# Windowed attention before two feed-forward layers: keys transposed straight into twelve pieces, scores masked and reduced for a duo at once

## The chip, the cores and the metric

The kernel runs on one core of one Trainium2 chip. A core has TensorE (PE) for matrix products, VectorE (DVE), ScalarE (ACT) and GpSimd (POOL) for element-wise work, and SyncE (SP), whose queue issues the transfers from and to memory. Products land in PSUM, eight banks of 512 fp32 values in each of 128 partitions; everything else lies in SBUF. The metric is the device time of one execution in microseconds: the median before is 644.8 us over three runs (640.82 to 644.95).

## The reference

Two batches of 8 heads, 768 tokens, 64 values a head. Each query sees the keys less than 16 tokens away, and beside them 24 summary keys, one for each block of 32 tokens: the maximum over the block, with log 32 added to its score; the summary value is the mean.

```python
k_sum = k.reshape(B, H, nb, block, D).max(axis=3)
v_sum = v.reshape(B, H, nb, block, D).mean(axis=3)
scores_l = scale * np.matmul(q, k.transpose(0, 1, 3, 2))
mask_l = np.abs(pos[:, None] - pos[None, :]) < window
scores_s = scale * np.einsum('bhsd,bhnd->bhsn', q, k_sum) + np.log(block)
scores_all = np.concatenate([np.where(mask_l, scores_l, -1e9), scores_s], axis=-1)
a = np.exp(scores_all - np.max(scores_all, axis=-1, keepdims=True))
a = a / (np.sum(a, axis=-1, keepdims=True) + 1e-09)
out = np.matmul(a, np.concatenate([v, v_sum], axis=2))
# then, on 1536 tokens x 512: h = relu(x @ w_in); x = h*h @ w_out  (512 -> 2048 -> 512)
# and: h = x @ w_in2; g = P(h) / Q(h); out = g @ w_out2            (512 -> 2048 -> 512)
```

The weights come as 8-byte numbers, whose two words ACT, DVE and POOL turn into a high and a low fp32 part; each product is three matmuls (high by high, high by low, low by high).

## The kernel before, in words

Attention works in **duos**: one pair of heads by 256 queries, four chunks (`c`) of 64 queries, the two heads side by side in 128 partitions. A batch is 12 duos in three groups of 256 tokens; a group's four duos give the 512 input rows of a feed-forward chunk of 256 tokens. There are 24 duos.

The keys of a head pair are loaded with token `p*6 + r` in partition `p` (L258), laid out anew by DVE or ACT (`k_rel`, R and A in the order below), transposed on PE six times 128 x 128 (`k_tr`, t), copied by ACT into a linear row of 768 tokens (`k_lin`, l), and from there by DVE or ACT into six overlapping windows `kt` of 184 columns, 160 window tokens with the 24 summary keys between them (`k_put`, c, C, B). The block maxima are taken from the linear row (L361).

A duo then goes through these steps. `d_t` and `d_z` (q, z) transpose and copy the queries; `d_s` (s) makes 4 x 120 scores in a PSUM bank; `d_m` (m) adds the mask, scales, negates and takes the minimum, one fused DVE instruction and a read-out a chunk (L444); `d_e` (e) is the exponential on ACT; `d_r` (r) the row sum, plus 1e-9, and reciprocal on DVE; `d_n` (n) the normalization on POOL; `d_p`, `d_b` (p, b or f) transpose and copy the weights; `d_o` (o) multiplies by the values; `d_x`, `d_y` (x, y) split the output into high and low parts, the input of the first layer (L546). `s_add` and `v_sum` (S, V) make the summary values on POOL and PE. T, D, W are the three steps that decode a piece of a weight.

The order of the first six duos and of the first weights is written out by hand (`START`, L22 to 27) and kept in that order on every engine; the loads that come first are listed in `LOADS`. What stands outside it, the constants of `build_consts` and all transfers, is placed by a scheduler that simulates the program. After the start the remaining duos are mixed into the first layer's steps. SP's queue issues all transfers in its order. The layers' passes: `FS` (L520) splits the first layer's 16 blocks into 5 and 11, and the first five run chunk by chunk beside attention.

Of the kernel before, what the change touches and what calls it, by code (L numbers as in the profile page):

```python
# [30 lines left out]
def tile_window_attention_moe_moe(  # L31
# [120 lines left out]
    TR = S // P  # L152
    TV = 8
    VP = S // TV
    bw = ap.tile([VP, LO + NB], F32, name="bw", bufs=1)
    qz = [ap.tile([P, 4, 2, LO], F32, name=f"qz{j}", bufs=1) for j in range(2)]
    kss = [ap.tile([P, NB], F32, name=f"kss{j}", bufs=1) for j in range(NP)]
    kt = [ap.tile([P, NQ, NKEY], F32, name=f"kt{j}", bufs=1) for j in range(NP)]
    vn = [[ap.tile([HK, 2, 2 * P], F32, name=f"vn{j}{i}", bufs=1) for i in range(2)] for j in range(2)]


    lins = [acc[:, j * KC * G:j * KC * G + S + LO] for j in (3, 2, 1, 0)]
# [4 lines left out]
    kst = const.tile([P, TR, 4, D], F32, tag="xh2", name="kst")  # L167
    vst = const.tile([P, 4, TV, D], F32, tag="xl2", name="vst")[0:VP]
# [17 lines left out]
    masks = {}  # L186

    def build_consts():
        make_identity(nc, ident)
        for lin in lins:  # L190
            nc.vector.memset(lin[:, 0:WIN], 0.0)
            nc.vector.memset(lin[:, WIN + S:], 0.0)
        for z in qz:
            nc.vector.memset(z[0:D, :, 1], 0.0)
            nc.vector.memset(z[D:P, :, 0], 0.0)
        m0 = ap.tile([P, 4, HK], F32, tag="pr", name="mask", bufs=NPR)
        m0 = m0.rearrange("p c t -> p (c t)")[:, 0:NKEY]
        nc.vector.memset(m0, 0.0)
        for c0, j0, n in ((0, 0, LO), (LO + NB, LO, WT - LO)):
            nc.gpsimd.affine_select(  # L200
                out=m0[:, c0:c0 + n], in_=m0[:, c0:c0 + n], pattern=[[1, n]],
                compare_op=ALU.is_ge, fill=NEG, base=j0 - 1, channel_multiplier=-1,
            )
            nc.gpsimd.affine_select(
                out=m0[:, c0:c0 + n], in_=m0[:, c0:c0 + n], pattern=[[-1, n]],
                compare_op=ALU.is_ge, fill=NEG, base=2 * WIN - 1 - j0, channel_multiplier=1,
            )
        nc.vector.memset(m0[:, LO:LO + NB], SC * math.log(BLK))

        mid = [ap.tile([P, HK], F32, name=f"mask_mid{h}", bufs=1) for h in range(2)]  # L210
        for h in range(2):
            for e in range(2):
                nc.vector.tensor_copy(
                    mid[h][e * LO:(e + 1) * LO], m0[h * LO:(h + 1) * LO, h * LO:h * LO + HK]
                )
        m1 = ap.tile([P, HK], F32, name="mask_first", bufs=1)
        nc.vector.tensor_copy(m1, mid[0])
        nc.vector.memset(m1[:, 0:WIN], NEG)
        m2 = ap.tile([P, HK], F32, name="mask_last", bufs=1)
        nc.vector.tensor_copy(m2, mid[1])  # L220
        nc.vector.memset(m2[:, HK - WIN:], NEG)
        masks.update({(i, h): mid[h] for i in range(NQ) for h in range(2)})
        masks[0, 0] = m1
        masks[NQ - 1, 1] = m2
        nc.vector.memset(bw, 1.0 / BLK)
        for sgn, base in ((1, 0), (-1, BLK - 1)):
            for c0 in (0, LO):
                nc.gpsimd.affine_select(
                    out=bw[:, c0:c0 + NB], in_=bw[:, c0:c0 + NB], pattern=[[-sgn * BLK, NB]],
                    compare_op=ALU.is_ge, fill=0.0, base=base - (sgn < 0) * (TV - 1),  # L230
                    channel_multiplier=sgn * TV,
                )
        nc.vector.memset(bw[:, NB:LO], 0.0)
# [3 lines left out]
    NPR = 3  # L237
# [7 lines left out]
    tog = [0]  # L245

    def early():

        tog[0] += 1
        return wp.tile([P, 2 * DM], F32, tag=("wh", "wl")[tog[0] % 2], name="early")  # L250
# [4 lines left out]
    def e_load(p):  # L255

        t = early()[:, 0:2 * TR * D]
        nc.sync.dma_start(out=t.rearrange("p (h c) -> p h c", h=2), in_=rows(k[0], 2 * p, 2, TR))  # L258
        ksrc[p] = t.rearrange("p (h r d) -> p h r d", r=TR, d=D)

    def s_load(bb, h, t):
# [3 lines left out]
            out=t.rearrange("p h r d -> p h (r d)"), in_=rows(v[bb], h, n, TV)  # L265
# [6 lines left out]
    def s_add(t, to=1):  # L272

        n = TV // 2
        while n >= to:
            for h in range(0, t.shape[1], 2):
# [8 lines left out]
    def k_rel(p, copy):

        t = early()[:, 0:2 * TR * D].rearrange("p (r h d) -> p r h d", r=TR, d=D)
        copy(out=t.rearrange("p r h d -> p h r d"), in_=ksrc[p])
        ksrc[p] = t

    late = tc.keep_in_program_order

# [20 lines left out]
    def v_load(g, hh, j):  # L313
# [5 lines left out]
        for dst, lo, n in ((t[0:LO, 0], t0, LO), (t[LO + NB:HK, 0], t0 + LO, BLK),  # L319
# [7 lines left out]
            for r, s, m in segs:  # L327
# [593 lines left out]
```

## Time and profile before

| | |
|---|---|
| runs, median (three) | 644.8 us (640.82 to 644.95) |
| profiled execution, its own time | 643.41 us |
| its span from first to last instruction | 641.3 us |
| PE busy | 613.1 us (96%) |
| DVE busy | 415.1 us (65%) |
| ACT busy | 408.2 us (64%) |
| POOL busy | 351.2 us (55%) |
| mean granted TensorE clock | 0.989 of full speed |

Busy time is the time in which an engine has an instruction under way. A span is cut into stages with different limits, so the shares above do not tell by themselves which engine decides; the rows further down cut it. The time of the profiled execution and its span differ by the 2.1 us that lie around the instructions.

### The profile page before, as it was taken

Reading aid. Unit: us, or ns where it says so; the run is one execution under the profiler, and the core shown is the slowest. Engines: PE = TensorE matmul, PEld = TensorE weight load, DVE = VectorE, ACT = ScalarE, POOL = GpSimd, SP = SyncE. Lnnn points to the kernel's source line nnn. Section 1 sums busy time; section 2 is a strip of 40 time slices with the busy share of each in tenths; the row PEclk is TensorE's granted clock in tenths of the full one; section 3 lists DMA queues with packets and bytes.
Section 4 is the critical chain, followed back from the end, with each engine's and each line's share of the span. In section 5 each row is a group of like instructions: output and inputs, shape, how many; then the busy total and the mean of one; then the engine's idle time right before and its main releaser. Section 6 shows DMA issues by size and latency. Waiting matters only on the chain.

```text
span 641.3 us, 9799 instructions
## 1 busy us (share of the span) xinstructions
PE 613.1 (96%) x3476; PEld 518.5 (81%) x3476; DVE 415.1 (65%) x850; ACT 408.2 (64%) x771; POOL 351.2 (55%) x363
## 2 busy tenths in 40 slices
PE   3788899999999999999999999999999999999996
PEld 3777788999998778888888888788888888888885
DVE  5788786764767652111126799988766977766672
ACT  5577675765666632222245799888878788777761
POOL 2548755543677742322266799955445765544441
PEclk9689999999999999999999999999999999999999
DMA  9856955221555640000005543310000000001011
GB/s 231 212 136 167 247 153 106 63 47 27 167 178 182 196 132 0 2 1 0 1 0 165 164 127 103 103 62 2 1 0 1 33 2 1 1 19 47 0 66 65
DMA packets 64783, 51.48 MB, mean 80 GB/s; under 512 B 40160, under 2 KB 57568, under 8 KB 64736
## 3 DMA queue, kind: packets, MB, share of 16 engines
q1 hardware_dynamic: 64736, 50.87, 28.3%
q8 instruction: 27, 0.44, 0.3%
q14 instruction: 20, 0.16, 0.1%
HBM read 47.71 MB, written 3.15 MB: 79 GB/s over the span
## 4 chain that ended last, share of the span: by engine, by line
PE 50%; DVE 7%; ACT 2%; POOL 2%; issue 1%; DMA 1%; DVEq 0%; POOLq 0%; ACTq 0%; SPq 0%
PE y L633 25%; PE h L546 25%; DVE wdec L131 2%; POOL wl L145 1%; POOL sl L610 1%; DVE h L595 1%; ACT wdec L120 1%; DMA wraw<-in_moe_w_out_dram 1%; DVE q L592 1%; DVE wdec L130 1%; DVE p L598 1%; DVE p L580 1%; DVE acc L659 1%; DVE p L579 1%; ACT sh L609 1%
## 5 line engine op out<-in xcount | busy, mean ns | idle before, releaser
L546 PE MATMUL h<-xh,wh 128*128 128x512 f32 (+1 forms) x444 | 162.3, 366 | 3.1 <-DVE r L576 1.6
L546 PE MATMUL h<-xh,wl 128*128 128x512 f32 (+1 forms) x444 | 161.1, 363 | 0.7 <-POOL wl L145 0.7
L546 PE MATMUL h<-xl,wh 128*128 128x512 f32 (+1 forms) x444 | 161.2, 363 | 0.0
L610 POOL TENSOR_TENSOR sl<-r,sh 128x512 fp32r<-128x512 f32 (+1 forms) x63 | 69.1, 1098 | 108.0 <-ACT sh L609 100.3
L567 POOL TENSOR_TENSOR q<-q,u 128x512 f32<-128x512 f32 x48 | 63.6, 1325 | 77.8 <-ACT q L564 75.5
L145 POOL TENSOR_TENSOR wl<-wdec,wh 128x512 fp32r<-128x512 f32 x64 | 86.5, 1360 | 27.5 <-ACT wh L144 24.9
L546 PEld LDWEIGHTS h<-xh,wh 128*128 128x128 f32 x444 | 83.4, 188 | 18.5 <-DVE r L576 2.3
L546 PEld LDWEIGHTS h<-xh,wl 128*128 128x128 f32 x444 | 83.4, 188 | 15.1 <-POOL wl L145 1.1
L576 DVE TENSOR_TENSOR r<-r,h 128x512 f32<-128x512 f32 (+1 forms) x63 | 35.0, 557 | 92.3 <-ACT r L559 92.1
L546 PEld LDWEIGHTS h<-xl,wh 128*128 128x128 f32 x444 | 83.5, 188 | 13.7
L633 PE MATMUL y<-sh,wh 128*128 128x512 f32 (+1 forms) x252 | 86.0, 344 | 0.8 <-ACT sh L609 0.8
L633 PE MATMUL y<-sh,wl 128*128 128x512 f32 (+1 forms) x252 | 85.1, 340 | 0.0
L633 PE MATMUL y<-sl,wh 128*128 128x512 f32 (+1 forms) x252 | 78.7, 341 | 0.2
L610 POOL TENSOR_TENSOR sl<-p,sh 128x512 fp32r<-128x512 f32 x48 | 64.9, 1352 | 21.1 <-ACT sh L609 17.1
L633 PE MATMUL y<-wl,sh 128*128 128x512 f32 x192 | 75.0, 390 | 0.0
L633 PE MATMUL y<-wh,sh 128*128 128x512 f32 x192 | 74.5, 390 | 0.0
L633 PE MATMUL y<-wh,sl 128*128 128x512 f32 x192 | 73.6, 389 | 0.0
L131 DVE SCALAR_TENSOR_TENSOR wdec<-wraw,wdec 128x512 int32<-128x512 int32 x64 | 64.7, 1014 | 1.4
L130 DVE TENSOR_SCALAR wdec<-wdec 128x512 int32<-128x512 int32 x64 | 46.0, 718 | 25.3 <-ACT wdec L120 25.2
L609 ACT CAST sh<-r 128x512 fp32r<-128x512 f32 (+1 forms) x63 | 32.4, 514 | 42.0 <-PE y L633 39.4
L559 ACT ACTIVATE r<-h 128x512 f32<-128x512 f32 (+1 forms) x63 | 31.0, 493 | 44.1 <-PE h L546 24.4
L144 ACT CAST wh<-wdec 128x512 fp32r<-128x512 f32 x64 | 39.3, 620 | 26.9 <-DVE wdec L131 26.8
(98 smaller groups left out, 1123.6 us busy)
## 6 DMA issues: line engine op xcount, KB each, us to landing
wraw<-in_moe_w_in_dram SPq DMA_DIRECT2D x32, 512.0 KB, 3.9
wraw<-in_moe_w_out_dram SPq DMA_DIRECT2D x32, 512.0 KB, 3.4
out_dram<-acc SPq DMA_DIRECT2D x12, 256.0 KB, 2.1
acc<-in_q_dram SPq DMA_DIRECT2D x10, 256.0 KB, 5.3
vn<-in_v_dram SPq DMA_DIRECT2D x20, 96.0 KB, 2.5
early<-in_k_dram SPq DMA_DIRECT2D x4, 384.0 KB, 4.9
early<-in_v_dram SPq DMA_DIRECT2D x4, 384.0 KB, 8.1
kst<-in_k_dram SPq DMA_DIRECT2D x8, 192.0 KB, 4.2
```

Of the source, the lines that this page charges most:

```text
L120: x = nc.scalar.activation(out=f32(t), in_=f32(r[:, :, 1]), func=AF.Prelu, scale=2.0 ** -112, alpha=-(2.0 ** 32))
L130: nc.vector.tensor_single_scalar(out=t, in_=t, scalar=3, op=ALU.logical_shift_left)
L131: nc.vector.scalar_tensor_tensor(out=t, in0=low, scalar=29, in1=t, op0=ALU.logical_shift_right, op1=ALU.bitwise_or)
L144: nc.scalar.copy(out=th[:, j], in_=t)
L145: nc.gpsimd.tensor_tensor(out=tl[:, j], in0=t, in1=f32(th[:, j]), op=ALU.subtract)
L546: nc.tensor.matmul(hq[g][:, 0:n], lhsT=w[:, 0, ws], rhs=x[:, part, ts], start=(part == 0 and j == 0), stop=(part == KC - 1 and j == 2),)
L559: nc.scalar.activation(out=r, in_=h, func=AF.Relu)
L567: nc.gpsimd.tensor_tensor(out=q_, in0=q_, in1=u_, op=ALU.mult)
L576: nc.vector.tensor_tensor(out=eq[g], in0=eq[g], in1=h, op=ALU.mult)
L609: nc.scalar.copy(out=sh[:, 0:n], in_=e)
L610: nc.gpsimd.tensor_tensor(out=sl[:, 0:n], in0=e, in1=f32(sh[:, 0:n]), op=ALU.subtract)
L633: nc.tensor.matmul(o, lhsT=lt, rhs=rt, start=(f == 0 and j == 0 and d * m % 512 == 0), stop=(f == FS[ps] - 1 and j == 2 and (d + 1) * m % ...
```

## The change

Keys are loaded with token `p*8 + r` in partition `p`, into partitions 2 to 97 of a tile whose partitions 0, 1 and 96 to 99 are zeroed first. Eight transposes of 100 columns give, in two banks, the tokens with 16 zeros before and after them. Two copies a pair, one for each bank, write from PSUM straight into twelve pieces of 96 window tokens, with the 24 summary keys behind them (120 columns); the linear row is gone, and the block maxima are taken from the pieces. The scale goes into the query copies. A duo's scores are masked by one addition of 480 elements from PSUM, and one reduction takes the four maxima, negated. The 1e-9 stands in a padded column of the score tile. Values are loaded in two transfers a tile for three, into slots of the weight pool. In `START` the copies of the second bank (k) are added and DVE and ACT exchange the first two relayouts.

```diff
-    "R1 A0 t0 R3 t1 q0 l0 l1 q1 S0 A2 c0 z0 t2 S1 s0 z1 c1 m0 T0 D0 l2 s1 q2 B0 q3 e0 V0 z2 "
...
+    "R0 A1 t0 R3 t1 q0 l0 k0 l1 k1 q1 S0 A2 c0 z0 t2 S1 s0 z1 c1 m0 T0 D0 l2 k2 s1 q2 B0 q3 "
...
+    early = [wp.tile([P, 2 * DM], F32, tag=("wh", "wl")[j % 2], name="early") for j in range(14)]
...
+    for t in [*early[0:4], kst]:
+        nc.vector.memset(t[0:K0], 0.0)
+        nc.vector.memset(t[VP:KP], 0.0)
...
     def e_load(p):
-        t = early()[:, 0:2 * TR * D]
-        nc.sync.dma_start(out=t.rearrange("p (h c) -> p h c", h=2), in_=rows(k[0], 2 * p, 2, TR))
+        t = early[p][0:KP].rearrange("p (h r d) -> p h r d", r=TR, d=D)
+        nc.sync.dma_start(
+            out=t[K0:K0 + VP].rearrange("p h r d -> p h (r d)"), in_=rows(k[0], 2 * p, 2, TR)
+        )
...
-    def k_lin(p, lin):
-        dst = lin[:, WIN:WIN + S].rearrange("p (t r) -> p r t", r=TR)
-        for (r0, n), pt in zip(CUT, pk.pop(p)):
-            nc.scalar.copy(
-                out=dst[:, r0:r0 + n], in_=pt[:, 0:n * P].rearrange("p (r t) -> p r t", r=n)
-            )
+    def k_lin(p, b, copy):
+        pt = pk[p][b]
+        src = pt[:, 0:4 * KP]
+        src = bass.AP(src.tensor, src.offset, [
+            list(src.ap[0]), [LO // TR, NWIN], [1, WT // TR], [KP, 4],
+        ])
+        dst = kt[p][:, :, 0:WT].rearrange("p w (t r) -> p w t r", r=TR)
+        copy(out=dst[:, :, :, 4 * b:4 * b + 4], in_=src)
...
-        for c in range(4):
-            nc.vector.tensor_tensor_reduce(
-                out=pr[:, c], in0=pt[:, c * HK:(c + 1) * HK], in1=masks[i + c // 2, c % 2],
-                op0=ALU.add, op1=ALU.min,
-                scale=-1.0 / SC, scalar=3e38, accum_out=mx[:, c:c + 1],
-            )
+        nc.vector.tensor_tensor(
+            out=s, in0=pt[:, 0:4 * HK].rearrange("p (c t) -> p c t", t=HK), in1=mk[:, m:m + 4],
+            op=ALU.add,
+        )
+        nc.vector.tensor_reduce(out=mx[:, 0:4], in_=s, axis=AX.X, op=ALU.max, negate=True)
...
         nc.vector.tensor_reduce(out=mx[:, 4:8], in_=pr, axis=AX.X, op=ALU.add)
-        nc.vector.tensor_scalar_add(rs, mx[:, 4:8], 1e-9)
-        nc.vector.reciprocal(out=rs, in_=rs)
+        nc.vector.reciprocal(out=rs, in_=mx[:, 4:8])
```

How the order of the instructions moves shows at three places. First, SP's queue from its start, before. `early` from `in_k` are the four key pairs (104 to 110), from `in_v` value pairs for the summaries, `vn` the windowed values, `wraw` raw weights, `acc` the queries.

```order
L306 DMA acc_78<-in_q_dram 128x4x64 x2
L258 DMA early_104<-in_k_dram 128x2x384
L258 DMA early_106<-in_k_dram 128x2x384
L258 DMA early_108<-in_k_dram 128x2x384
L258 DMA early_110<-in_k_dram 128x2x384
L328 DMA vn10_97<-in_v_dram 16x4x64
L328 DMA vn10_97<-in_v_dram 48x4x64
L328 DMA vn10_97<-in_v_dram 32x4x64
L328 DMA vn10_97<-in_v_dram 96x4x64
L108 DMA wraw_116<-in_moe_w_in_dram 128x4x256
```

Behind these stand two value pairs, the second query half, two value pairs, another four pieces of `vn`, and the first raw piece of w_out. Now the same queue of the change, from its sixth row on. Ahead of these rows stand the first query half, three pieces of windowed values and the first key pair (early_98); the other three pairs are 99, 100 and 101.

```order
L108 DMA wraw_135<-in_moe_w_in_dram 128x4x256
L269 DMA early_106<-in_v_dram 96x2x512
L269 DMA early_107<-in_v_dram 96x2x512
L294 DMA acc_78<-in_q_dram 128x4x64
L246 DMA early_99<-in_k_dram 96x2x512
L294 DMA acc_78<-in_q_dram 128x4x64
L269 DMA early_108<-in_v_dram 96x2x512
L269 DMA early_109<-in_v_dram 96x2x512
L246 DMA early_100<-in_k_dram 96x2x512
```

Behind these come three pieces of windowed values, the first raw piece of w_out, and then the fourth key pair:

```order
L315 DMA early_110<-in_v_dram 16x4x64
L315 DMA early_110<-in_v_dram 80x4x64
L315 DMA early_110<-in_v_dram 96x4x64
L110 DMA wraw_146<-in_moe_w_out_dram 128x1024
L246 DMA early_101<-in_k_dram 96x2x512
```

The four key pairs stood together at the head; now each stands behind other loads, the fourth behind all of them.

Second, DVE from the last constants on, before: the two relayouts, then the first pair's maxima and copies.

```order
L288 COPY early_197<-early_106 128x2x6x64
L288 COPY early_209<-early_110 128x2x6x64
L361 TENSOR_REDUCE kss0_87<-acc_78 128x24
L368 COPY kt0_91<-acc_78 128x2x64
L368 COPY kt0_91<-acc_78 128x2x96
L369 COPY kt0_91<-kss0_87 128x2x24
L418 COPY qz0_85<-pt_219 64x4x64
```

And DVE of the change from its first relayout on.

```order
L254 COPY early_102<-early_98 100x2x8x64
L227 MEMSET bw_84 96x96
L214 COPY mask_114<-mask_114 64x96
L216 COPY mask_114<-mask_114 128x96
L217 COPY mask_114<-mask_114 128x4x96
L218 MEMSET mask_114 128x16
L219 MEMSET mask_114 128x16
L254 COPY early_105<-early_101 100x2x8x64
L341 COPY kt0_91<-pk_191 128x12x12x4
L341 COPY kt1_92<-pk_202 128x12x12x4
L348 TENSOR_REDUCE kss0_87<-kt0_91 128x24
L354 COPY kt0_91<-kss0_87 128x4x24
```

The relayout of the fourth pair (early_101) still stands ahead of the first pair's copies; the mask copies now stand ahead of it too, and ahead of all this stand ten memsets of the key tiles.

Third, POOL of the change, where the mask's and the mean weights' selections now stand behind the four value additions; before, they stood ahead of them.

```order
L283 TENSOR_TENSOR early_106<-early_106 96x2x256
L283 TENSOR_TENSOR early_107<-early_107 96x2x256
L283 TENSOR_TENSOR early_108<-early_108 96x2x256
L283 TENSOR_TENSOR early_109<-early_109 96x2x256
L205 AFFINE_SELECT mask_114<-mask_114 64x96
L222 AFFINE_SELECT bw_84<-bw_84 96x24
L209 AFFINE_SELECT mask_114<-mask_114 64x96
L222 AFFINE_SELECT bw_84<-bw_84 96x24
```

The mask copies on DVE (L214) wait for the second selection of the mask, and so for the last value addition.

## Rows read from the trace of the kernel before

**Rows 1.** Stretches: start:end, width, busy per engine (instructions), PE clock, DMA share, GB/s.

```profile
0.00:43.19 43.19, 27.68 (x201) 24.69 (x201) 29.19 (x121) 26.52 (x63) 16.60 (x39) 0.84 0.77 187
43.19:120.00 76.81, 70.25 (x665) 63.89 (x661) 61.72 (x209) 54.56 (x142) 50.33 (x82) 1.00 0.64 157
120.00:617.00 497.00, 496.01 (x2535) 414.37 (x2535) 314.01 (x507) 320.39 (x556) 277.79 (x238) 1.00 0.20 61
9.69:39.53 29.84, 22.34 (x161) 19.66 (x159) 21.77 (x86) 20.81 (x55) 12.53 (x21) 0.79 0.80 186
```

**Rows 2.** Timeline of DVE: start, duration, instruction, idle time before it and its releaser.

```profile
9.69 0.56 DVE L288 COPY early<-early 128x768 f32<-128x768 f32 x1 [2.08 <-DMA early<-in_k_dram]
...
14.18 0.28 DVE L444 CUSTOM_DVE_ANT_0 pr<-pss,mask_first 128x120 f32<-128x120 f32 x1
...
14.99 0.94 DVE L130 TENSOR_SCALAR wdec<-wdec 128x512 int32<-128x512 int32 x1
...
18.45 0.43 DVE L418 COPY qz<-pt 64x256 f32<-64x256 f32 x1 [1.79 <-ACT qz L418]
...
24.46 0.43 DVE L418 COPY qz<-pt 64x256 f32<-64x256 f32 x1 [2.23 <-ACT qz L418]
...
39.53 0.42 DVE L514 TENSOR_TENSOR xl<-pav,xh 128x256 fp32r<-128x256 f32 x1
```

**Rows 3.** Waits of DVE from 9.69 to 39.53 us: total, times, longest.

```profile
DVE qz L418 <- ACT qz L418: 7.1, 5, 2.2
```

**Rows 4.** Timeline of PE and POOL: the second query half and the last values arrive.

```profile
17.49 0.90 PE L410 MATMUL pt<-ident,acc 128*128 128x128 f32 x3 [0.41 <-DMA acc<-in_q_dram]
...
20.69 1.30 POOL L278 TENSOR_TENSOR early<-early 96x512 f32<-96x512 f32 x1 [0.36 <-DMA early<-in_v_dram]
```

**Rows 5.** First w_out piece: its issue on SP; transfers issued 16.5 to 17, us to landing.

```profile
16.52 0.35 SPq L110 DMA_DIRECT2D wraw<-in_moe_w_out_dram  x1
...
wraw<-in_moe_w_out_dram SPq DMA_DIRECT2D x1, 512.0 KB, 7.1
```

**Rows 6.** Two stretches of the start, columns as in the first group.

```profile
10.00:20.00 10.00, 6.27 (x38) 5.35 (x37) 7.60 (x31) 7.43 (x19) 3.91 (x3) 0.83 1.15 235
20.00:30.00 10.00, 7.09 (x35) 6.90 (x34) 7.58 (x27) 4.53 (x12) 5.31 (x11) 0.67 0.95 243
```

**Rows 7.** Groups on DVE (9.69 to 39.53; last three whole or early): count, busy, mean ns.

```profile
L288 DVE COPY early<-early 128x768 f32<-128x768 f32 x1 | 0.6, 559 | 2.1 <-DMA early<-in_k_dram 2.1
L368 DVE COPY kt<-acc 128x128 f32<-128x128 f32 (+3 forms) x12 | 3.6, 342 | 0.0
L461 DVE TENSOR_REDUCE mx<-pr 128x4 f32<-128x480 f32 x4 | 2.5, 637 | 0.0
L462 DVE TENSOR_SCALAR rs<-mx 128x4 f32<-128x4 f32 x4 | 1.1, 287 | 0.2
...
L645 DVE COPY acc<-y 128x512 f32<-128x512 f32 x1 | 0.7, 662 | 0.0
L659 DVE TENSOR_TENSOR acc<-y,acc 128x512 f32<-128x512 f32 x24 | 15.3, 684 | 12.8 <-PE y L633 12.7
L198 DVE MEMSET mask<- 128x184 f32 x1 | 0.2, 212 | 0.1
```

**Rows 8.** Groups on ACT, 0 to 120 us.

```profile
L352 ACT COPY acc<-pk 128x512 f32<-128x512 f32 x8 | 8.8, 1106 | 5.8 <-PE pk L343 3.5 <-DVE kt L368 2.3
L483 ACT COPY pp<-ptp 120x512 f32<-120x512 f32 x14 | 8.1, 581 | 4.8 <-PE ptp L479 4.8
```

**Rows 9.** Groups on DVE, 60 to 160 us: key copies of the second batch.

```profile
L368 DVE COPY kt<-acc 128x384 f32<-128x384 f32 (+1 forms) x8 | 4.8, 636 | 0.0
```

**Rows 10.** Waits of PE, 43 to 125 us: total, times, longest.

```profile
PE h L546 <- ACT wh L144: 1.2, 1, 1.2
PE pk L343 <- DMA kst<-in_k_dram: 0.9, 1, 0.9
```

More of the change, by code (lines that the diff above doesn't have):

```diff
@@ L184, in free @@
         banks.append(held.pop(id(t)))
-    masks = {}
+    mk = ap.tile([P, 6, HK], F32, name="mask", bufs=1)
     def build_consts():
         make_identity(nc, ident)
-        for lin in lins:
-            nc.vector.memset(lin[:, 0:WIN], 0.0)
-            nc.vector.memset(lin[:, WIN + S:], 0.0)
         for z in qz:
@@ L208, in build_consts @@
[L208 to L224, printed above, removed]
+        for t in prs:
+            nc.vector.memset(t[:, :, HK:], 1e-9)
+        m = mk[0:LO, 1, 0:WT]
+        nc.vector.memset(m, 0.0)
+        nc.gpsimd.affine_select(
+            out=m, in_=m, pattern=[[1, WT]], compare_op=ALU.is_ge, fill=NEG, base=-1,
+            channel_multiplier=-1,
+        )
@@ L225, in build_consts @@
         nc.vector.memset(bw, 1.0 / BLK)
         for sgn, base in ((1, 0), (-1, BLK - 1)):
[L227 to L233, printed above, removed]
+            nc.gpsimd.affine_select(
+                out=bw[:, WT:], in_=bw[:, WT:], pattern=[[-sgn * BLK, NB]],
+                compare_op=ALU.is_ge, fill=0.0, base=base - (sgn < 0) * (TR - 1),
+                channel_multiplier=sgn * TR,
+            )
@@ L243, in at @@
         return g // (NQ // 2), 2 * (g % (NQ // 2)) + j, p, j
[L245 to L250, printed above, removed]
+    late = tc.keep_in_program_order
     def rows(src, h, n, t):
@@ L255, in e_load, with k_rel, k_load @@
     def e_load(p):
[L257 to L259 removed]
+        t = early[p][0:KP].rearrange("p (h r d) -> p h r d", r=TR, d=D)
+        nc.sync.dma_start(
+            out=t[K0:K0 + VP].rearrange("p h r d -> p h (r d)"), in_=rows(k[0], 2 * p, 2, TR)
+        )
+        ksrc[p] = t
+    def k_rel(p, copy):
+        t = early[4 + p][0:KP].rearrange("p (r h d) -> p r h d", r=TR, d=D)
+        copy(out=t.rearrange("p r h d -> p h r d"), in_=ksrc[p])
+        ksrc[p] = t
+    def k_load(hh):
+        for h in range(4):
+            late(nc.sync.dma_start(
+                out=kst[K0:K0 + VP, :, h], in_=k[1, 4 * hh + h].rearrange("(p r) d -> p r d", r=TR)
+            ))
+        for j in range(2):
+            ksrc[2 * hh + j] = kst[:, :, 2 * j:2 * j + 2]
     def s_load(bb, h, t):
@@ L280, in s_add @@
                 )
-                if n == TV // 2 and t.shape[1] > 2:
+                if n == TR // 2 and t.shape[1] > 2:
                     tc.keep_in_program_order(x)
             n //= 2
[L285 to L291, printed above, removed]
-    def k_load(hh):
-        for h in range(4):
-            late(nc.sync.dma_start(
-                out=kst[:, :, h], in_=k[1, 4 * hh + h].rearrange("(p r) d -> p r d", r=TR)
-            ))
-        for j in range(2):
-            ksrc[2 * hh + j] = kst[:, :, 2 * j:2 * j + 2]
     def q_load(g, hs=slice(0, H)):
@@ L781, in tile_window_attention_moe_moe @@
     LEFT = 4
-    some, rest = slice(0, 2), slice(2, NQ)
+    some, rest = slice(0, 4), slice(4, NWIN)
     def v_last(h, copy):
```

138 lines of the change are left out of this document (68 added, 70 removed), and 6 rows, old and new, of the table START.

## The prediction

> **What bounds the kernel now.** I read the stages first. [Rows 1] cuts the span at the first matmul of the first feed-forward layer (43.19 us). From 120 to 617 us TensorE is busy 496.01 of 497.00 us: whatever reaches it late there is late at the end, and nothing there can be made up. From 43.19 to 120 us it idles 76.81 - 70.25 = 6.6 us, and before 43.19 us it idles 43.19 - 27.68 = 15.5 us. So the change, which touches attention alone, can move the end in two ways: by the moment at which the first layer starts, and by these 6.6 us.
>
> What sets that moment is the hand-ordered start, and in it VectorE (DVE). In [rows 2], the timeline of DVE, its first instruction that waits for a late input is the relayout of the fourth key pair, R3, at 9.69 us; after it follow the first maxima m0 (14.18), the query copies z2 (18.45) and z3 (24.46), and at 39.53 the first subtraction xl of an attention output. The first layer starts 3.7 us behind it, with the fourth duo's values. Over these 29.84 us DVE works 21.77 us (the fourth row of [rows 1]) and waits 8.1; 7.1 of these are before the query copies [rows 3]. The waits at z2 (1.79) and z3 (2.23) come from transfers: the query half that TensorE got at 17.49 us, and the value sums that stand ahead of the fourth transposes on TensorE, whose last input reached GpSimd at 20.69 us [rows 4].
>
> **What the order does to the keys.** This is the largest term and the diff does not say it. The keys are now loaded into rows 2 to 97 of a tile whose rows 0, 1 and 96 to 99 are zeroed by DVE first; rows 96 and 97 are written by both, so each key load waits for a memset. The scheduler therefore moved the loads: in the queue of before the four stand behind the first query half; now three of them are spread, and the fourth stands as number 20. Ahead of it are the values, both query halves, and two raw weight pieces.
>
> The transfers up to and with it are the same set as the first 22 of before, which end with the first piece of w_out: two query halves, four key pairs, two pieces of windowed values, one w_in piece, four value pairs, one w_out piece. That piece was issued at 16.52 us and took 7.1 us to land [rows 5], so at 23.6 us. The queue moved 235 to 243 GB/s over 10 to 30 us, its engines full [rows 6]. Equal bytes at an equal rate: the fourth key pair lands at 23.6 us, and R3, which waits for it and for nothing later, starts **13.9 us later** (23.6 - 9.69). Everything on DVE from the first key copy on is queued behind R3, and through it the score matmuls, exponentials, normalization on GpSimd and the first layer. The second and third pair land earlier and wait behind R3 for their second halves' copies.
>
> **The other edits, on DVE from R3 to the first xl.** Durations from [rows 7].
> - R3 copies 1024 elements in place of 768: 559 ns x 1024/768 = 745, +0.2 us.
> - The copies out of the linear keys fall away, twelve of them: -3.6 us.
> - Four copies of 576 elements straight from PSUM come in. The lower bound is the plain PSUM copy, 662 ns for 512, so 0.75 us. The upper bound comes from ScalarE [rows 8]: writing every sixth element takes 1106 ns where a plain copy of 512 takes 581, so 0.75 x 1.9 = 1.43. The new copy reads with a step of 100 elements but writes runs of four, so it lies between, and I take 1.0: +4.0 us (3.0 to 5.7).
> - Scores, five duos (m0 to m4). Before: from 14.18 to 14.99 us in [rows 2], 0.81 us for the four fused instructions with their read-outs. After: one addition of 480 elements from PSUM, 684 ns x 480/512 = 0.64, and a maximum like the row sum, 0.64 us; less the few hundredths by which neighbours overlap, 1.3 us. +0.5 each, +2.5 us.
> - The added 1e-9 now comes from a padded column: four additions of 1.1 us in all fall away, -1.1 us.
>
> Together +2.0 us of work (0.2 - 3.6 + 4.0 + 2.5 - 1.1), so 23.8 us from R3 to xl.
>
> [...]
>
> [...] No row here shows a read of PSUM with a step.
>
> Which waits stay? z2's and z3's (4.0 us) go, since query and values have long landed at 23.6; of the other 4.1 I keep 3.2, above all those before z4 and z5, which hang on chains through ScalarE and TensorE, and drop the rest, because ScalarE has 14 us to get ahead. Then xl starts at 23.6 + 23.8 + 3.2 = 50.6 us against 39.53: **+11.1 us**, and the first layer with it.
>
> **Off the path.** Ten memsets of 1024 to 2048 elements open DVE's queue: 1.2 us for each 1024 by the 212 ns of 184 elements [rows 7], some 14 us in all, or less if only their start is dear. They end before 16 us, R0 follows. The mask's two selections on GpSimd now stand behind the four value additions. The value loads now end where as many bytes had landed as with the query half at 17.49 us before, so the last addition (1.30 us) ends near 19 and the mask copies near 21. All that is covered by the wait for the fourth key pair; were that gone, the mask would hold R3 at 21. TensorE gets 32 transposes of 100 columns for 24 of 128, ScalarE four copies of 576 for eight of 512 and 256, neither of which ends last. The windowed values take two transfers for three, same bytes. In the second batch DVE loses the copies out of the linear keys, 4.8 us [rows 9], and pays 0.2 us a duo for the scores less the addition that falls away (0.5 - 0.3); ScalarE carries the new copies.
>
> **Given back.** Of the 6.6 us of idle after 43.19 us, 0.9 wait for keys and 1.2 for weights [rows 10], which a later start meets better prepared, and the lighter DVE helps the rest a little. I take 1.5.
>
> **The sum**: 11.1 - 1.5 = +9.6 us on the profiled execution's 643.41 us, so **653.0 us**; that execution stands 1.4 us under the median of the runs, 644.8, and between their ends. Its own range: without any kept wait, with copies at 0.75 and 2.1 given back, +11.1 - 3.2 - 1.0 - 2.1 = +4.8, 648.2; with copies at 1.43 and nothing given back +12.8, 656.2.
>
> **The rivals.**
> - *The idle takes it*, the case on the other side. The mechanism is DVE's relief of 4.8 us in the second batch, between 60 and 120 us: with it TensorE could run without a gap up to 120 us, and the whole 6.6 us of idle would come off, +11.1 - 6.6 = +4.5, 647.9, which is not slower by what can be measured, and 643.7 with the cheap bounds above (+6.9 - 6.6). It decides from 4.7 us given back. For it: DVE works 61.72 of the 76.81 us. Against: the waits there are short chains over several engines, and these move along with the start. 0.17.
> - *Nothing is absorbed.* The start is a chain, not DVE's sum: each step finds the next engine cold. The granted clock is 0.67 from 20 to 30 us even in the busier start of before [rows 6], and a TensorE that idles up to 24 us will be slower after. Then the full 13.9, plus the dear copies' 1.7: 659.0. 0.17.
> - *The queue's order is not the order of landing.* The loads share 16 engines; if the fourth pair overtakes weights and values issued before it, the mask's 21 us take its place and the time falls by up to 2.6 us, to 650.4, at the edge of what can be told. For it: a slower early part of the queue would leave several transfers under way at once. Against: in before the query half and the last values reached their engines in the order of issue (17.49, then 20.69 us), and the rate leaves no room. 0.08.
>
> The forecast keeps 0.58. Differences within 1% (6.4 us, so 637.0 to 649.8) are what a measurement of this kernel can hardly tell from none. Slower by more: nine tenths of the forecast and the second rival, 0.52 + 0.17 = 0.69. Within: the rest of the forecast, nearly all of the first rival and half of the third, 0.06 + 0.16 + 0.04 = 0.26, and the other half of the third goes to both ends: slower 0.69, faster 0.05. The range reaches from inside the first rival to just past the second, 645 to 660.
>
> **What would show it.** The profile after should have R3 waiting for a key load until about 23.6 us; m0 near 29 in place of 14.18; the first layer near 54.3 in place of 43.19; 120 to 617 us as full as before; a DVE addition near 0.64 us and a copy from PSUM of 0.75 to 1.43 us. R3 before 20 us would make the prediction wrong at its root; R3 at 23.6 with the first layer before 47 would show that I kept too many waits; both as forecast with an end near 644 would mean that the idle was given back.

## The result, and the profile after

The changed kernel takes **651.68 us** (median of four runs, 650.38 to 652.35), the kernel before beside it 644.85 (640.82 to 644.95): ratio 1.0119, 95% interval 1.0076 to 1.0162, so 6.8 us slower: just over 1%, with an interval that reaches a little below. Forecast were 653.0 us and a range of 645 to 660. The profiled execution took 650.38 us with a span of 648.6; that is 7.0 and 7.3 us more than the profiled execution of before. Of all executions reported below, one is in a slow state and stands in no ratio, the 646.99 us of the split zeros with fused scores.

The stages first, in the form of [rows 1], cut at the first matmul of the first layer, which is now at 55.22 us in place of 43.19; the last row runs from R3, the relayout of the fourth key pair, to the first `xl`. Columns: start:end, width, busy time (instructions) of PE, PE's weight loads, DVE, ACT and POOL, granted PE clock, DMA share, GB/s.

```profile
0.00:55.22 55.22, 27.11 (x208) 24.27 (x208) 40.30 (x76) 22.74 (x55) 15.47 (x35) 0.96 0.68 154
55.22:120.00 64.78, 60.96 (x589) 57.09 (x588) 51.79 (x105) 47.59 (x125) 47.60 (x73) 0.98 0.80 179
120.00:624.30 504.30, 503.50 (x2616) 422.49 (x2615) 324.17 (x475) 325.70 (x573) 281.45 (x247) 1.00 0.19 60
24.93:51.23 26.30, 20.29 (x159) 18.43 (x160) 22.56 (x44) 14.39 (x41) 6.78 (x17) 0.94 0.36 88
```

TensorE has the same 27 us of work before the first layer as in [rows 1], but 28.1 us of idle time around it (55.22 - 27.11) in place of 15.5. From 120 us on it is as full as before. So the whole difference lies in the start, less what comes back between 55 and 120 us.

The timeline of DVE in the start answers to [rows 2]: start, duration, instruction, idle time before it and its releaser.

```profile
1.07 0.91 DVE L715 MEMSET early<- 2x1024 f32 x1 [1.07 <-PEq L889]
...
9.25 0.91 DVE L716 MEMSET early<- 4x1024 f32 x1 [0.25 <-issue]
...
12.87 1.76 DVE L716 MEMSET kst<- 4x2048 f32 x1 [0.47 <-issue]
...
16.53 0.62 DVE L254 COPY early<-early 100x1024 f32<-100x1024 f32 x1
...
21.19 0.20 DVE L214 COPY mask<-mask 64x96 f32<-64x96 f32 x1 [3.94 <-POOL mask L209]
...
24.93 0.69 DVE L254 COPY early<-early 100x1024 f32<-100x1024 f32 x1 [2.87 <-DMA early<-in_k_dram]
25.53 1.41 DVE L341 COPY kt<-pk 128x576 f32<-128x576 f32 x2
...
30.66 0.66 DVE L424 TENSOR_TENSOR pr<-pss,mask 128x480 f32<-128x480 f32 x1 [0.60 <-PE pss L409]
31.35 0.65 DVE L428 TENSOR_REDUCE mx<-pr 128x4 f32<-128x480 f32 x1
...
51.23 0.42 DVE L493 TENSOR_TENSOR xl<-pav,xh 128x256 fp32r<-128x256 f32 x1
```

Three things hold DVE one after another: the ten memsets until 14.6 us, the mask (21.19) and the fourth key load (24.93). R3 starts 15.2 us later than its 9.69 of before, and the first `xl` 11.7 us later. The load in question is issued on SP's queue behind the raw w_out piece; first the timeline of SP, then the transfers issued around it (KB, us to landing).

```profile
15.17 0.35 SPq L110 DMA_DIRECT2D wraw<-in_moe_w_out_dram  x1
15.88 0.31 SPq L246 DMA_DIRECT2D early<-in_k_dram  x1
```

```profile
wraw<-in_moe_w_out_dram SPq DMA_DIRECT2D x1, 512.0 KB, 8.5
early<-in_k_dram SPq DMA_DIRECT2D x1, 384.0 KB, 9.0
```

15.88 + 9.0 is R3's 24.9: the wait is for this transfer and nothing else. The last memset of its tile ended at 10.2 us (9.25 + 0.91), 5.7 us before the load was issued; so in this run the place in the queue holds the load, not the zeroing itself.

The costliest DVE groups of the changed steps from R3 to the first `xl` (count, busy, mean ns, idle before), the answer to [rows 7], and one of ACT between 60 and 125 us, the answer to [rows 8]:

```profile
L424 DVE TENSOR_TENSOR pr<-pss,mask 128x480 f32<-128x480 f32 x5 | 3.3, 657 | 1.0 <-PE pss L409 0.9
L428 DVE TENSOR_REDUCE mx<-pr 128x4 f32<-128x480 f32 x5 | 3.3, 653 | 0.2
L341 DVE COPY kt<-pk 128x576 f32<-128x576 f32 x4 | 2.9, 744 | 0.0
```

```profile
L341 ACT COPY kt<-pk 128x576 f32<-128x576 f32 x8 | 4.9, 634 | 0.1
```

DVE's waits for query copies in this stretch, 7.1 us in [rows 3], are down to:

```profile
DVE qz L398 <- ACT qz L398: 2.0, 3, 1.2
```

The pair for the scores costs 1.31 us, and the copies straight from PSUM 0.74. That is a plain copy's rate: 1.29 ns an element, as the 662 ns for 512 in [rows 7]; on ACT 634 ns for 576 elements stand beside 581 for 512 in [rows 8].

### The profile page after: what moved, and what is told of

Same layout as the page of the kernel before. It is cut to its first block, busy times and chain, and to the rows that moved or that the text cites. A ratio compares the mean times of both kernels' runs of the same rounds, so it can differ in the third digit from the quotient of the medians.

```text
span 648.6 us, 9605 instructions
## 1 busy us (share of the span) xinstructions
PE 610.7 (94%) x3492; PEld 519.4 (80%) x3492; DVE 426.4 (66%) x668; ACT 402.8 (62%) x763; POOL 351.0 (54%) x359
## 4 chain that ended last, share of the span: by engine, by line
PE 62%; DVE 0%; ACT 0%; DVEq 0%; issue 0%
PE y L612 32%; PE h L525 31%; DVE acc L638 0%; ACT wdec L120 0%; DVEq L902 0%; ACT sh L588 0%; ACT r L538 0%
## 5 line engine op out<-in xcount | busy, mean ns | idle before, releaser
L145 POOL TENSOR_TENSOR wl<-wdec,wh 128x512 fp32r<-128x512 f32 x64 | 87.8, 1381 | 23.0 <-ACT wh L144 22.9
L525 PEld LDWEIGHTS h<-xh,wl 128*128 128x128 f32 x444 | 83.7, 189 | 13.9
L131 DVE SCALAR_TENSOR_TENSOR wdec<-wraw,wdec 128x512 int32<-128x512 int32 x64 | 66.6, 1041 | 1.5
L130 DVE TENSOR_SCALAR wdec<-wdec 128x512 int32<-128x512 int32 x64 | 47.3, 740 | 20.5 <-ACT wdec L120 20.3
L448 POOL TENSOR_SCALAR pr<-pr,rs 128x120 f32<-128x120 f32 x96 | 36.9, 404 | 42.7 <-DVE rs L442 36.8
```

What stands on the lines that cost most here:

```text
L130: nc.vector.tensor_single_scalar(out=t, in_=t, scalar=3, op=ALU.logical_shift_left)
L131: nc.vector.scalar_tensor_tensor(out=t, in0=low, scalar=29, in1=t, op0=ALU.logical_shift_right, op1=ALU.bitwise_or)
L145: nc.gpsimd.tensor_tensor(out=tl[:, j], in0=t, in1=f32(th[:, j]), op=ALU.subtract)
L448: nc.gpsimd.tensor_scalar(out=pr[:, c, 0:HK], in0=pr[:, c, 0:HK], scalar1=rs[:, c:c + 1], scalar2=1.0, op0=ALU.mult, op1=ALU.mult,)
L525: nc.tensor.matmul(hq[g][:, 0:n], lhsT=w[:, 0, ws], rhs=x[:, part, ts], start=(part == 0 and j == 0), stop=(part == KC - 1 and j == 2),)
```

## The experiments

Ratios are to the kernel before, run beside each on the same chip (its medians there lie between 642.8 and 643.7 us). The runs come from several chips, so the ratios compare better than the medians. Where two variants differ by 2 us, the trace is the better witness: executions of one kernel scatter by 2 to 9 us, while two kernels below whose start is that of the changed one and that of before put their first layers at 55.91 and 43.41 us, beside 55.22 and 43.19. Three traces (the order held, the split zeros, the load on DVE) are of executions 2.6 to 4.2 us above the median of their kernel; they take 597.2 to 597.5 us from the first layer to the end, the changed kernel 593.4, so what they take longer lies behind the start. In the diffs, "..." marks what is left out.

**The key order alone.** The kernel before, with nothing changed but the list of its first loads.

```diff
-"q0 k0 k1 k2 k3 n2 w0 v0 v1 q1 v2 v3 n0 w1 Q1 w2 n1 n3"
+"q0 n2 k0 w0 v0 v1 q1 k1 v2 v3 k2 n0 w1 k3 Q1 w2 n1 n3"
```

> The kernel before with one line changed: the list of first loads names the keys in the places where the changed queue has them (q0 n2 k0 w0 v0 v1 q1 k1 v2 v3 k2 n0 w1 k3). Nothing else of the change is in it. Theory: R3 at 23.6 to 25 us in place of 9.69, z2 and z3 no longer wait for transfers, the first layer 11 to 12 us late, near 54.5. At the end 650 to 651 if a late start is partly made up whatever the kernel, 654 to 656 if only the lighter DVE of the change made it up. Rival (the key order costs nothing by itself): 643 to 645.

Measured: 655.18 us (652.65 to 655.56), ratio 1.0158, 1.0136 to 1.0179. Two rows of its trace, R3 on DVE and the windows from its first layer (54.49 us) on:

```profile
24.46 0.56 DVE L288 COPY early<-early 128x768 f32<-128x768 f32 x1 [7.49 <-DMA early<-in_k_dram]
```

```profile
54.49:629.10 574.61, 566.08 (x3197) 478.40 (x3194) 376.46 (x716) 374.71 (x698) 328.57 (x320) 1.00 0.26 74
```

R3 is as late as in the changed kernel, the first layer comes 11.3 us late, and the end 12.1 us (span 653.4): more than the whole change. So the late order is enough for the whole loss, and of a late start nothing comes back by itself: TensorE idles 8.5 us after its first layer, before 573.81 - 566.26 = 7.6.

**The order held, the zeros kept.** In the changed kernel all first loads are kept on SP's queue in the order of the list (one of them shown), the keys each behind their memsets.

```diff
-        nc.sync.dma_start(
+        late(nc.sync.dma_start(
             out=t[K0:K0 + VP].rearrange("p h r d -> p h (r d)"), in_=rows(k[0], 2 * p, 2, TR)
-        )
+        ))
...
```

> The change with its first loads pinned in the order of the list, keys at the head; the ten memsets on DVE stay, and the keys wait for them. This parts the two ways in which the zeroing can cost: through the scheduler's order of the loads, or through DVE's own time (the memsets ended at 14.6 us, the first relayout started at 16.5). Theory (the order was the larger part): R3 at 17 to 19 us in place of 24.93, the first layer at 50 to 51.5, the end at 647 to 649. Rival (DVE's memsets, and the query half and values that now stand behind waiting keys, cost as much): 651 to 653.

Measured: 646.46 us (645.26 to 650.69), ratio 1.0062, 1.0037 to 1.0086. DVE's timeline, then PE's first matmul of the first layer:

```profile
16.53 1.22 DVE L256 COPY early<-early 100x1024 f32<-100x1024 f32 x2
...
18.28 0.20 DVE L216 COPY mask<-mask 64x96 f32<-64x96 f32 x1 [0.42 <-POOL mask L211]
```

```profile
51.53 0.39 PE L527 MATMUL h<-xh,wh 128*128 128x256 f32 x1
```

R3 now runs right behind R0 without a wait of its own, once DVE is through the memsets (14.6 us) and the constants behind them. The key loads, at the head of SP's queue, stand behind the memsets:

```profile
SPq L248 <- DVE early L718: 7.4, 4, 2.0
```

The first layer comes 3.7 us earlier than in the changed kernel, and the time is just under the 647 to 649 expected. Against the split zeros below, where neither the order nor a memset holds the keys, the first layer is 10.1 us late in the changed kernel and 6.4 here: with the order put right 3.7 come back, and the memsets, which then hold back both the loads and DVE, keep the rest. The ratios (1.0119, 1.0062, 0.9961) say the same. These are no fixed shares, since R3 waits for whichever ends last; the run before shows that late keys alone are enough.

**Neither: keys in partitions 0 to 95, no zeroed tile.** The zeros around the tokens come from the transposes: each is a product with a unit matrix shifted by two columns.

```diff
...
-            nc.tensor.transpose(
-                out=pt[:, r % 4 * KP:(r % 4 + 1) * KP], in_=src[:, r],
-                identity=ident[0:KP, 0:KP],
-            )
+            nc.tensor.matmul(
+                pt[:, r % 4 * KP:(r % 4 + 1) * KP], lhsT=src[:, r], rhs=idw, start=True, stop=True
+            )
...
```

> The change with one thing taken away: keys are loaded into partitions 0 to 95, no tile is zeroed, and the eight transposes become products with a 96 x 100 unit matrix shifted by two columns, which writes the zeros itself. Key loads wait for nothing and stand at the head of the queue again. Theory (the key order and its memset cause the loss): R3 back near 9.7 us, the first layer near 43 us in place of 55.22, the loss gone. If what was given back after the start (12.0 us late at the first layer, 7.3 at the end of the profiled runs) came from the lighter DVE, it now shows as a gain: 640 to 641. If it was only work that a later start finds prepared, the time is that of before, 643 to 645. Rival (the loss lies in the other edits, the two score instructions and the copies from PSUM): 649 to 652, with R3 early all the same.

Measured: 647.13 us (645.43 to 648.32), ratio 1.0046, 1.0028 to 1.0063. R3 starts at 11.40, the first layer at 46.50; the time fits none of the forecasts. The edit is not clean: the products cost more than the transposes. PE's group of them up to the first layer, here and in the changed kernel (count, busy, mean ns, idle before):

```profile
L334 PE MATMUL pk<-idw,early 96*128 96x100 f32 x64 | 12.9, 386 | 7.4 <-DVE early L260 7.4
```

```profile
L328 PE MATMUL pk<-ident,early 100*128 100x100 f32 x32 | 5.6, 347 | 21.7 <-DVE bw L227 17.3 <-DVE kt L341 3.4 <-ACT early L254 0.9
```

Twice the matmul instructions for the same blocks, 7.3 us more before the first layer and 4.0 in the second batch (7.8 for 3.8). It shows the early start, not its worth.

**The same with the four fused score instructions** (their edit is two experiments down).

> The first and third together: keys early, no memsets, fused scores. If both reasons hold and add, 2 us under the early keys alone: 638 to 639, faster than both kernels. If DVE has slack in the start once the keys are early (it waits for the second query half and the values there), the fused scores bring nothing on top: the same time as the early keys alone.

Measured: 645.42 us (643.65 to 648.78), ratio 1.0025, 1.0011 to 1.0039: 1.7 us under the run without, first layer at 44.87, 1.6 us earlier. The step is near the 2 us expected; the level of 638 to 639 is missed, since the products are still in it.

**Split zeros.** The keys lie in partitions 0 to 95, and only 96 and 97 are zeroed, rows that no load writes; one short extra transpose a bank puts the leading zeros in place. No load waits for a memset, and the transposes stay transposes.

```diff
-    KP = VP + 2 * WIN // TR
+    KP = VP + WIN // TR
...
-            out=t[K0:K0 + VP].rearrange("p h r d -> p h (r d)"), in_=rows(k[0], 2 * p, 2, TR)
+            out=t[0:VP].rearrange("p h r d -> p h (r d)"), in_=rows(k[0], 2 * p, 2, TR)
...
+            if r % 4 == 0:
+                nc.tensor.transpose(
+                    out=pt[:, 0:K0], in_=src[VP:KP, r], identity=ident[VP:KP, VP:KP]
+                )
...
```

> The change with the zero rows moved out of the loads' way: keys in partitions 0 to 95, zeros in 96 and 97 alone, written by one memset a tile (two on DVE, two on GpSimd, that of the second batch later on GpSimd); two extra transposes of two columns a pair bring the leading zeros. Transposes, not products, so TensorE's work is as in the change. Theory: the early-keys run kept the loss because its products by the shifted unit matrix were dear on TensorE (PE busy 620.2 against 610.7 us), in the start as in the second batch; with transposes R3 is at 9.7 to 10 us, the first layer at 43 to 44.5, and the lighter DVE's give-back (12.0 - 7.3 = 4.7 us in the change) is a gain: 639 to 641. Rival (the score step and the copies from PSUM cost about what the lighter DVE gives, so nothing is left once the keys are early): 643 to 645.

Measured: 640.68 us (637.81 to 644.6), ratio 0.9961, 0.994 to 0.9982, faster than either kernel. DVE's timeline, then PE's groups of transposes up to the first layer:

```profile
6.39 0.69 DVE L254 COPY early<-early 98x1024 f32<-98x1024 f32 x1
11.62 0.69 DVE L254 COPY early<-early 98x1024 f32<-98x1024 f32 x1 [4.54 <-DMA early<-in_k_dram]
...
17.75 0.66 DVE L428 TENSOR_TENSOR pr<-pss,mask 128x480 f32<-128x480 f32 x1
```

```profile
L332 PE MATMUL pk<-ident,early 98*128 98x98 f32 x32 | 7.3, 383 | 0.0
L329 PE MATMUL pk<-ident,early 2*128 2x2 f32 x8 | 2.1, 259 | 7.2 <-DVE early L254 7.2
```

The zeros are the cause: without them on loaded rows R3 is back near its old place, the first layer at 45.13, and of the time 10 to 11 us are gone (1.6% by the ratios). The rest of the change (pieces straight from PSUM, one mask addition and what goes with them) is together a small gain. Not shown is the reason that the expectation gave for the early keys' 647 us: TensorE is busy 618.9 us here, hardly less than the 620.2 with the products.

**The fused score instructions back in the changed kernel.**

```diff
-        nc.vector.tensor_tensor(
-            out=s, in0=pt[:, 0:4 * HK].rearrange("p (c t) -> p c t", t=HK), in1=mk[:, m:m + 4],
-            op=ALU.add,
-        )
-        nc.vector.tensor_reduce(out=mx[:, 0:4], in_=s, axis=AX.X, op=ALU.max, negate=True)
+        for c in range(4):
+            nc.vector.tensor_tensor_reduce(
+                out=pr[:, c, 0:HK], in0=pt[:, c * HK:(c + 1) * HK], in1=mk[:, m + c],
+                op0=ALU.add, op1=ALU.min,
+                scale=-1.0, scalar=3e38, accum_out=mx[:, c:c + 1],
+            )
...
```

The exponential on ACT, left out here, takes the sign back with a scale of -1.

> The change with its score step alone undone: four fused instructions and read-outs for the one addition and one maximum; loads and memsets stay. By the rows (0.81 us for four fused, 1.30 for the pair) the first layer starts 2 to 2.5 us earlier than 55.22 and the end is at 649 to 650. [...]

Measured: 649.21 us (647.64 to 650.68), ratio 1.0080, 1.0061 to 1.0099. R3 is where it was (24.86), the first layer at 53.09 in place of 55.22. So merging a duo's scores costs 2.1 us over the five duos ahead of the first layer, 0.43 each, and by the medians 2.5 at the end, though there the two intervals overlap.

**The fused score instructions with split zeros.**

> The same with the four fused score instructions of before. The late-key run with them was 2.5 us faster than the change; here DVE waits for the second query half in the start, so between nothing and 2.5 us under the split zeros alone: 637 to 640 by the theory, 641 to 644 by the rival.

Measured: 641.05 us (637.08 to 646.99), ratio 0.9974, 0.995 to 0.9997: no gain over the split zeros alone, as the rival had it, though the first layer starts at 40.95. The last pair of runs below shows why.

**R3 later.** The changed kernel with R3 moved in the hand-written order.

```diff
-    "R0 A1 t0 R3 t1 q0 l0 k0 l1 k1 q1 S0 A2 c0 z0 t2 S1 s0 z1 c1 m0 T0 D0 l2 k2 s1 q2 B0 q3 "
+    "R0 A1 t0 t1 q0 l0 k0 l1 k1 q1 S0 A2 c0 z0 t2 S1 s0 z1 c1 m0 T0 D0 l2 k2 R3 s1 q2 B0 q3 "
```

> The changed kernel with the relayout of the fourth key pair (R3) moved in the hand-written order from ahead of the first key copies to behind those of the third pair; no work is left out. My theory, that everything of DVE stood behind R3 (24.93 us) and that without it the mask copies (21.2 us) set the start: the first maxima m0 at 27 to 28 us instead of 30.66, the first layer 2.5 to 3 us earlier than 55.22, about 52.5, and the end near 649. Rival, that the fourth pair's landing itself holds the first layer, since the fourth duo needs it and the wait only moves: m0 earlier, the first layer and the end unchanged, 651 to 652.

Measured: 649.33 us (647.94 to 650.04), ratio 1.0091, 1.0071 to 1.0111. DVE's timeline:

```profile
21.64 0.20 DVE L214 COPY mask<-mask 64x96 f32<-64x96 f32 x1 [4.38 <-POOL mask L209]
...
22.41 0.74 DVE L341 COPY kt<-pk 128x576 f32<-128x576 f32 x1
...
27.53 0.66 DVE L424 TENSOR_TENSOR pr<-pss,mask 128x480 f32<-128x480 f32 x1 [0.60 <-PE pss L409]
...
30.52 0.68 DVE L254 COPY early<-early 100x1024 f32<-100x1024 f32 x1
```

The first maxima move 3.1 us forward, to the place that the mask copies leave them, the first layer 2.2 (53.00). The end moves with it, by 2.4 us. The queue behind R3 and the mask as the next bound are both shown, and so is that the fourth pair is not needed so early itself.

**DVE's load in the second batch, from both sides.** Does the lighter DVE give time back there? First the kernel before, with the second batch's eight window copies (4.8 us, [rows 9]) moved from DVE to ACT; then the changed kernel, with its eight copies from PSUM moved from ACT to DVE.

```diff
-            groups.append([lambda r=r: k_put(r // 2, lins[0])])
+            groups.append([lambda r=r: k_put(r // 2, lins[0], copy=nc.scalar.copy)])
```

> The kernel before the change, with only the window copies of the keys of the second batch moved from DVE to ACT (eight copies, 4.8 us of DVE). No work is left out; the start is untouched. If DVE's relief in the second batch is what the change gets back between 55 and 120 us (4.7 us there): about 2 to 4 us faster than before, 640 to 642. If it is not DVE's load that ends last there, the same as before, 643 to 645, or a little slower where ACT's copies come late.

```diff
-                lambda r=r: k_tr(r // 2), lambda r=r: k_lin(r // 2, 0, nc.scalar.copy),
-                lambda r=r: k_lin(r // 2, 1, nc.scalar.copy),
+                lambda r=r: k_tr(r // 2), lambda r=r: k_lin(r // 2, 0, nc.vector.tensor_copy),
+                lambda r=r: k_lin(r // 2, 1, nc.vector.tensor_copy),
```

> The change with the eight copies from PSUM of the second batch moved from ACT to DVE, 8 x 0.74 = 6 us that fill what DVE lost there (4.8 us of copies out of the linear keys). The start is untouched. If the give-back after the first layer's start comes from the lighter DVE, most of it goes: 653 to 656. If it comes from anything else, the time stays at 651 to 652.5, or falls with ACT's relief.

Measured: before with the relief 642.22 us (638.81 to 645.38), ratio 0.9979, 0.9958 to 1.0000; the changed kernel with the load 652.77 (651.43 to 655.41), ratio 1.0146, 1.0123 to 1.0169. Windows from the first layer on, of the first and of the second:

```profile
43.41:616.00 572.59, 567.44 (x3196) 481.26 (x3195) 371.88 (x702) 379.96 (x711) 327.77 (x320) 0.99 0.26 74
```

```profile
55.91:629.10 573.19, 567.27 (x3203) 481.53 (x3202) 377.93 (x587) 367.89 (x690) 329.83 (x320) 0.99 0.26 73
```

TensorE's idle time falls from 7.6 to 5.2 us with the relief and rises from 4.6 to 5.9 with the load. What falls away with the relief is a wait of the first layer for a tile of DVE, before and with the relief:

```profile
PE h L546 <- DVE r L576: 1.6, 2, 1.0
```

```profile
PE h L546 <- DVE r L576: 0.2, 1, 0.2
```

Both runs point the same way, but the times differ by only 1 to 2 us each and lie between the forecasts; the intervals do not part them from no effect, and the second trace is of the slowest of its seven executions: supported, not shown.

**A better order for the split zeros, without and with the fused scores.** R3 behind the third pair's transposes, the fourth pair's transposes ahead of the value sums on PE.

```diff
-    "R0 A1 t0 R3 t1 q0 l0 k0 l1 k1 q1 S0 A2 c0 z0 t2 S1 s0 z1 c1 m0 T0 D0 l2 k2 s1 q2 B0 q3 "
-    "e0 V0 z2 m1 C1 r0 t3 e1 S2 l3 k3 z3 S3 Z0 X2 c2 s2 n0 W0 u0 c3 w0 r1 p0 s3 b0 m2 n1 C3 p1 "
+    "R0 A1 t0 t1 q0 l0 k0 l1 k1 q1 S0 A2 c0 z0 t2 R3 S1 s0 z1 c1 m0 T0 D0 l2 k2 s1 q2 B0 q3 "
+    "e0 t3 z2 m1 C1 r0 V0 e1 S2 l3 k3 z3 S3 Z0 X2 c2 s2 n0 W0 u0 c3 w0 r1 p0 s3 b0 m2 n1 C3 p1 "
```

> The kernel with the split zeros (keys in partitions 0 to 95, the two zero partitions written apart, 640.7 us) with R3 behind the third pair's transposes in the order and the fourth pair's transposes ahead of the value sums on PE. No work is left out. If its start was held by the two waits that its trace shows (R3 4.54 us for its load, the third key copy 2.64 us for transposes behind the value sums), the first layer moves from 45.1 to about 42 us and the end to 637 to 639. If these waits are replaced by the next late input, the query half, the start and the end stay, 640 to 642.

> The kernel before it in this call, with the four fused maxima and their read-outs in place of one addition and one maximum for each duo. If the pair costs 0.5 us a duo on the path (five duos before the first layer), the first layer comes about 2 us earlier and the end at 635 to 638. If, as with the split zeros in the old order, DVE is not what ends last in a prompt start, no difference beyond the scatter, 637 to 641.

Measured: 639.99 us (638.85 to 640.93), ratio 0.9950, 0.9931 to 0.9969, and with the fused scores 640.31 (636.61 to 644.16), ratio 0.9948, 0.9926 to 0.9970. The first layers start at 43.27 and 41.38 us. In the first the order helps the start by 1.9 us of the 3 expected, and the time by 0.7, less than the scatter. In the second the 1.9 us more are lost again, so the time is as in the expectation's second case, but not for its reason. The longest wait of PE after its first layer, and the windows around it (the columns of the first table):

```profile
PE pk L332 <- DMA kst<-in_k_dram: 2.8, 1, 2.8
```

```profile
50.00:56.00 6.00, 5.95 (x57) 5.05 (x55) 5.88 (x20) 5.28 (x14) 3.89 (x7) 1.00 0.72 162
56.00:58.00 2.00, 0.00 (x0) 0.00 (x0) 1.97 (x10) 1.45 (x4) 2.00 (x4) 0.86 1.31 197
58.00:67.00 9.00, 8.26 (x49) 7.49 (x49) 3.57 (x7) 3.45 (x8) 4.55 (x9) 0.50 0.97 203
```

and without the fused scores:

```profile
58.00:67.00 9.00, 7.39 (x68) 6.28 (x67) 7.05 (x16) 5.61 (x14) 7.98 (x15) 1.00 1.00 185
```

With the shorter score steps the scheduler puts the full transposes of the second batch's first keys so early that they start at 58.7 us, when the keys land, in place of 66.7. TensorE stands there before, waits 2.8 us, and has a granted clock of 0.50 for the next 9 us: 49 matmuls where the other kernel does 68. The split zeros with fused scores in the old order show the same wait (2.3 us). That this takes back the whole gain is read from these rows; no run brings those keys earlier.

The version with the better order and one addition has the lowest median and scatters by 2 us: 0.5% under the kernel before, and 11.7 us under the changed one by the medians.

## Why the prediction was right, point by point

**The keys' order and R3: right, 1.3 us early.** R3 was forecast at 23.6 and came at 24.93, 15.2 us late in place of 13.9. The reasoning by equal bytes held: the fourth pair lands behind everything ahead of it in the queue (the w_out piece, issued at 15.17 us, at 23.7, the pair at 24.9). What it missed is the rate at the queue's head. The windows of the first stretches, now and then of before (the last column is GB/s):

```profile
0.00:5.00 5.00, 0.00 (x0) 0.00 (x0) 3.16 (x4) 1.28 (x1) 0.78 (x8) 1.00 0.49 101
5.00:10.00 5.00, 0.00 (x0) 0.00 (x0) 3.97 (x5) 0.00 (x0) 0.00 (x0) 1.00 1.02 266
...
15.00:20.00 5.00, 2.70 (x17) 2.73 (x18) 1.94 (x11) 2.12 (x3) 1.93 (x2) 1.00 1.11 232
```

```profile
0.00:5.00 5.00, 0.00 (x0) 0.00 (x0) 2.68 (x20) 1.28 (x1) 2.26 (x16) 1.00 0.53 133
5.00:10.00 5.00, 2.97 (x15) 3.00 (x16) 1.42 (x7) 2.68 (x4) 0.00 (x0) 1.00 1.11 318
```

After ten microseconds the queue is (32 + 52) x 5 us = 0.42 MB behind, 1.8 us at 232 GB/s, which more than covers the 1.3; why its head was slower was not tried. The rival that landing does not follow the queue is refuted, and its second half, the mask as the next bound at 21 us, is shown by the run with R3 later. One reading of [rows 2] was loose and changes no term: before, R3 was not the first to wait for a late key, since the other relayout on DVE, at 7.05 us, had waited 1.42 us for its own.

**From R3 to the first xl: right.** Forecast 23.8 us of work and 3.2 of waits, found 22.6 and 3.7, and a start of the first layer at 55.22 for 54.3.

- The copies straight from PSUM were sized between 0.75 and 1.43 us, 1.0 taken; they cost 0.74. That is 1.0 us of the missing work. Reads at a step of 100 elements took 744 ns for 576 on DVE, where a plain copy took 662 for 512, and 634 for 576 on ACT. The dear 1106 ns of ACT in [rows 8] thus came, by elimination, from its scattered writes and not from the reads of PSUM; no run tried the writes alone.
- The pair of instructions for the scores, 1.3 us forecast, is 0.66 + 0.65, and the run with the four fused ones gives 0.43 us a duo back, 0.5 forecast. Before, the four fused instructions with their read-outs took 0.81 us, since each starts 0.2 us behind the one before it while its record lasts 0.28. The second of them, after the first at 14.18 in [rows 2]:

```profile
14.39 0.28 DVE L444 CUSTOM_DVE_ANT_0 pr<-pss,mask_mid 128x120 f32<-128x120 f32 x1
```

**The term that was mis-sized: given back.** I took 1.5 us and found 12.0 - 7.3 = 4.7 (the first layer's delay less that of the span; by the medians it is 12.0 - 6.8 = 5.2, and single executions scatter by 2 us and more). Of it 2.9 are TensorE's idle time after the first layer (7.55 before, 569.08 - 564.46 = 4.62 after) and 1.8 its busy time. My first reason, that a later start meets weights and keys better prepared, is wrong. With the late order alone nothing was given back, and both waits of [rows 10] stayed, as PE's waits in that run show:

```profile
PE pk L343 <- DMA kst<-in_k_dram: 1.1, 1, 1.1
PE h L546 <- ACT wh L144: 1.0, 1, 1.0
```

What came back is owed to the change's other edits. My second reason, the lighter DVE in the second batch, was named and thought small; moving those copies off DVE in the kernel before took 2.4 us of idle time, but left both waits of [rows 10] (1.3 and 0.8 us), which are gone in the changed kernel; which of its edits removes them is open. The 1.8 us of busy time remain open too: the durations of TensorE's groups from the first layer on sum to 986.7 us before and 987.6 after, so there is no less work; by the profile its instructions overlap more, and which edit does that was not tried.

The three errors are +1.3 (R3), -0.7 (work and waits) and -3.2 (given back); the first layer to `xl` distance adds 0.3. Together -2.3, and 9.6 - 2.3 = 7.3, the change of the span. So part of the nearness of 653.0 to 651.68 is luck: a give-back three times the size assumed was set off in part by a start 0.9 us later than forecast.

**The rivals.** That the idle takes it was nearer than its chance of 0.17: 4.7 us came back, 2.9 of them idle time, just the point that was named as decisive; only since the start was 12.0 late and not 11.1 did the median stay above 1%, and the interval of the ratio leaves that side open. That nothing is absorbed is refuted, and its reason too: TensorE, late as it was, was granted 0.94 from R3 to the first `xl`, 0.79 in [rows 1].

## What to carry to other kernels

Here zeroing rows that a load also writes tied the load to the memset (7.4 us of waiting for memsets at the four key loads, with the order held), and since a scheduler places the transfers, the tie showed as another order of the whole queue (R3 at 24.93 us for 9.69): read the order of the loads before costing the instructions. Keys sent late cost their whole delay where nothing else was changed (11.3 us at the first layer, 12.1 at the end); "it will catch up" needs a wait with a name and a reason to go. And an earlier start was worth only as much as the next input was early: the wait of 2.8 us for the second batch's keys and the granted clock of 0.50 in the 9 us behind it stand where a first layer at 41.38 us for 43.27 was lost again.

## What was not expected of the hardware

- DVE's memsets of two to four partitions by 1024 elements took 0.91 us each and those by 2048 took 1.76, with 0.25 and 0.47 us between them, and one of 64 partitions by 256 took 0.27: the time went with the length of the rows, not with their number.
- The wait of 2.8 us for keys was followed by 9 us at a granted clock of 0.50, in which TensorE did 49 matmuls for 68.
- A product with a unit matrix was twice the instructions of a transpose of about the same size: for the first batch's keys 64 of 386 ns in the early-keys run, against 32 of 383 in the split zeros, whose start is as early.
